# Down-score matmuls of a head quad spread among its local-score matmuls

## The chip, the core and the metric

The kernel runs on one core of a Trainium2 chip. Its engines are PE (matrix multiplication, with a separate record for the loading of weights, PEld), DVE (vector work), ACT (activation functions), POOL (general vector work, and the issue of some DMAs) and SP (the issue of the other DMAs). The metric is the device time of one execution in microseconds (us). All cited lines of code are lines of the kernel before.

## The reference

Eight batches of eight heads with 576 positions of 64 features go through two kinds of attention whose outputs are added. The down attention averages queries, keys and values over groups of four positions, attends over the resulting 144, and repeats each output four times. The local attention lets a position see only positions less than four away. The sum goes, as 4608 tokens of 512 features, through two matrix products with an activation between them.

```
q_d, k_d, v_d = mean over groups of 4 positions
out_up    = repeat(softmax(q_d k_d^T / 8) v_d, 4)
out_local = softmax(where(|i-j| < 4, q k^T / 8, -1e9)) v
x = (out_up + out_local) as 4608 x 512
h = x w_in                                   # 512 -> 2048
out = (h * sigmoid(1.702 h)) w_out           # 2048 -> 512
```

## The kernel before

**Two kinds of work share PE.** The two matrix products run in 9 groups (g = 0 to 8) of 512 tokens. For a group, `mm1` (L702) computes 16 chunks of h, each from 4 matmuls of 512 columns (L687), and ACT applies the activation (`silu`, L698). Then `mm2` (L711) computes 4 blocks of 128 tokens, each from 16 matmuls of 512 columns (L743), and ACT copies each result out (`store`, L728). The attention of batch b = g + 1 is cut into steps that are inserted between these matmuls. Batch 0's attention is done ahead of all groups and by other functions; the diff doesn't change it.

**Steps and places.** `attention` (L644) returns the steps of a batch as a list, and the list `POS` (L772) gives the place of each: places below 16 stand ahead of that chunk of `mm1`, and place 16 + n ahead of the n-th matmul of `mm2`. For g of 1 or more the steps are: score matmuls of quad 0 at 13, their exponentials at 16, scores and exponentials of quad 1 together at 33, the products with the values of head pairs 0 and 1 at 42, of pairs 2 and 3 at 53, and transposes and merges at 62 and 71. Batch 1 runs in group 0 with its own list `POS_0`, where the first steps are at 16, 18 and 27. All engines' orders are as written out in the program: no scheduler moves anything.

**A score burst.** Heads are taken in quads, of which there are two per batch (`qd` 0 and 1). A head's 64 features lie in 32 partitions with two values each (`a` 0 and 1), so a quad's four heads (`r`) fill the four row groups of the PE array. `scores` (L362) computes the local scores in 5 blocks of keys (`i`), each with 2 halves of 64 keys (`par`): 16 matmuls of 32 rows, 64 columns of weights and 60 columns of queries per block, 80 in all. They go to the 8 array tiles in turn, four row groups by two column halves. `scores_d` (L384) computes the down scores in 3 chunks of 48 keys (`kc`): 8 matmuls of 32 rows, 64 columns of weights and 144 columns of queries per chunk, 24 in all. Head r uses only the column half r % 2, so these use 4 of the 8 tiles. Every matmul has a weight load of its own. `s_pe` (L647) issues all 80 local ones and then all 24 down ones.

**Tiles and their release.** Scores go to PSUM, where three double-bank tiles `PA` are handed out in turn by `ps_tile` (L72). A burst takes two for the local scores (`sp`) and a third for the down scores (`sd`). The second burst of a batch takes the same three as the first in the same order, so its local matmuls wait for the exponentials of the first burst's local scores (`exp_local`, L403, two instructions) and its down matmuls for the exponential of the down scores (`exp_down`, L409). ACT runs these three in this order, behind the last activation of `mm1` and the load of a function table (L653). DVE then masks the local ones (L417). The next user of the tiles is `av` (L419), with matmuls at L434 and L456.

**Where the operands come from.** DVE transposes the loaded keys and queries to `kT` and `qT` (L276). POOL averages them to `kdT` and `qdT` (L294, L297), the ones of quad 0 first, then converts the batch's values (L308), then does quad 1, then averages the values (L314, L317). In batch 1 DVE and POOL share the averaging.

Of the kernel before, what the change touches and what calls it, by code (L numbers as in the profile page):

```python
# [19 lines left out]
def kernel(  # L20
# [51 lines left out]
    def ps_tile(n=None):  # L72
        if n is None:
            n = turn["a"] % 3
            turn["a"] += 1
        return PA[n]
# [275 lines left out]
    def bar_others(sp):  # L352
        for r in range(4):
            nc.tensor.matmul(
                sp[r // 2][:, r % 2, 0:300],
                lhsT=id128,
                rhs=off[:, None, :].to_broadcast([128, 5, 60]),
                start=True, stop=True,
                skip_group_check=True,
            )  # L360

    def scores(b, qd, barred=False, sp=None):  # L362
        sp = sp or [ps_tile(), ps_tile()]
        if barred:
            bar_others(sp)
        for i in range(5):
            for a in range(2):
                for par in range(2):
                    for r in range(4):
                        rows = slice(32 * r, 32 * r + 32)  # L370
                        k0 = 114 * i + KSTART[par]
                        q0 = 114 * i + QSTART[par]
                        nc.tensor.matmul(  # L373
                            sp[r // 2][64 * par : 64 * par + 64, r % 2, 60 * i : 60 * i + 60],
                            lhsT=kT[b, qd][rows, k0 : k0 + 64, a],
                            rhs=qT[b, qd][rows, q0 : q0 + 60, a],
                            start=(a == 0 and not barred),
                            stop=(a == 1 or barred),
                            tile_position=(32 * r, 64 * par),
                            skip_group_check=barred,  # L380
                        )
        return sp

    def scores_d(b, qd, sd=None):  # L384
        sd = sd or ps_tile()
        bank = banks(sd)
        for kc in range(3):
            for a in range(2):
                for r in range(4):
                    rows = slice(32 * r, 32 * r + 32)  # L390
                    j = r % 2
                    nc.tensor.matmul(  # L392
                        bank[r // 2][64 * j : 64 * j + 64, SD * kc : SD * kc + SD],
                        lhsT=kdT[qd][rows, 48 * kc : 48 * kc + 64, a],
                        rhs=qdT[b, qd][rows, :, a],
                        start=(a == 0), stop=(a == 1),
                        tile_position=(32 * r, 64 * j),
                    )
        return sd

    def exp_local(qd, sp):
        for u in range(2):
            nc.scalar.activation(  # L403
                out=es[2 * qd + u][:, :, 0:300], in_=sp[u][:, :, 0:300],
                func=AF.Exp, scale=inv_sqrt_d,
            )

    def exp_down(qd, sd):
        nc.scalar.activation(  # L409
            out=eds[qd][:, :, 0:432], in_=sd[:, :, 0:432],  # L410
            func=AF.Exp, scale=inv_sqrt_d / 16.0,
        )

    def mask_local(qd):
        for u in range(2):
            ev = es[2 * qd + u][:, :, 0:300]
            nc.vector.tensor_tensor(out=ev, in0=ev, in1=mask, op=ALU.mult)  # L417

    def av(b, hp, n=None):  # L419
        o = ps_tile(n)  # L420
        av_local(b, hp, o)
        av_down(b, hp, o)
        return o

    def banks(t):
        return t if t is PM else [t[:, u, :] for u in range(2)]
# [37 lines left out]
    def normalise(o):  # L464
        y = work.tile([128, 2, 7, D], BF16, name="y", tag="y", bufs=4)
        rc = work.tile([128, 2, 7, 1], FP32, name="rc", tag="rc")
        for xs in (slice(0, 1), slice(1, 2)) if o is PM else (slice(0, 2),):
            n = xs.stop - xs.start
            ov = (o[xs.start][:, None, :] if o is PM else o)[:, :, 0:455].rearrange(
                "p x (c e) -> p x c e", e=65  # L470
            )
            nc.vector.reciprocal(rc[:, xs], ov[:, :, :, 64:65])  # L472
            nc.vector.tensor_tensor(  # L473
                out=y[:, xs], in0=ov[:, :, :, 0:D],
                in1=rc[:, xs].to_broadcast([128, n, 7, D]), op=ALU.mult,
            )
        return y

    def transp(y, n=None):
        x = ps_tile(n)  # L480
        for i in range(5):
            for par in range(2):
                for j in range(2):
                    pos = j if par == 0 else 1 - j
                    c0 = 0 if (par == 1 or i == 0) else 3
                    c1 = 60 if (par == 0 or i == 4) else 57
                    nc.tensor.matmul(  # L487
                        x[64 * j : 64 * j + 64, par, 57 * i + c0 : 57 * i + c1],
                        lhsT=y[64 * pos : 64 * pos + 60, par, i, :],
                        rhs=ident(pos, 60, c0, c1),  # L490
                        start=True, stop=True,
                        tile_position=(64 * pos, 64 * j),
                    )
        for c2, xx in ((0, 0), (0, 1), (1, 0)):
            for j in range(2):
                pos = j if xx == 0 else 1 - j
                nc.tensor.matmul(  # L497
                    x[64 * j : 64 * j + 64, xx, 288 + 48 * c2 : 336 + 48 * c2],
                    lhsT=y[64 * pos : 64 * pos + 48, j, 5 + c2, :],
                    rhs=ident(pos, 48, 0, 48),  # L500
                    start=True, stop=True,
                    tile_position=(64 * pos, 64 * j),
                )
        return x
# [91 lines left out]
    def copy_od(x):  # L596
        od = work.tile([128, S], FP32, name="od", tag="od")
        for xx, t0, n in ((0, 0, 96), (1, 96, 48)):
            nc.scalar.copy(  # L599
                out=od[:, 4 * t0 : 4 * (t0 + n)].rearrange("p (t f) -> p t f", f=4),  # L600
                in_=x[:, xx, 288 : 288 + n, None].to_broadcast([128, n, 4]),
            )
        return od
# [40 lines left out]
    def attention(b, slots=None):  # L644
        st = {}

        def s_pe(qd):  # L647
            st["s", qd] = scores(b, qd)
            st["d", qd] = scores_d(b, qd)

        def s_act(qd):
            if qd == 0:
                nc.scalar.preload_act_table_set("exp_and_others")  # L653
            exp_local(qd, st["s", qd])
            exp_down(qd, st["d", qd])
            if qd == 1:
                nc.scalar.preload_act_table_set("silu_and_others")
            mask_local(qd)

        def s1():  # L660
            s_pe(1)
            s_act(1)

        def avn(*hps):
            def f():
                for hp in hps:
                    st["o", hp] = av(b, hp, slots and slots[hp % 2])
                for hp in hps:
                    st["y", hp] = normalise(st["o", hp])
            return f  # L670

        def tr(*hps):
            def f():
                for hp in hps:
                    st["x", hp] = transp(st["y", hp], slots and slots[hp % 2])
                for hp in hps:
                    od = copy_od(st["x", hp])
                    merge(b, hp, st["x", hp], od)
            return f

        first = [lambda: s_pe(0), lambda: s_act(0), s1, avn(0, 1)]
        if b == 1:
            return first + [tr(0), tr(1), avn(2, 3), tr(2), tr(3)]
        return first + [avn(2, 3), tr(0, 1), tr(2, 3)]
# [84 lines left out]
        for f in steps.get(n, ()):  # L769
            f()  # L770

    POS = [13, 16, 33, 42, 53, 62, 71]  # L772
    POS_0 = [16, 18, 27, 48, 52, 57, 66, 70, 75]
    VDP_0 = 44

    o, y, x = {}, {}, {}
# [28 lines left out]
    prep_1("k", 0, 0)  # L805
    prep_1("q", 0, 0)
    sp = scores(0, 0, barred=True, sp=PA[0:2])
    exp_local(0, sp)
    pool_1(0, 0, "k", nc.vector)
# [5 lines left out]
    for n in range(22):  # L815
        nc.tensor.matmul(
            PM[1][:, 0:256], lhsT=zero16[:, 0:128], rhs=zero16, start=True, stop=True
        )
    exp_down(0, scores_d(0, 0, PA[2]))
    make_up()  # L820
    sp = scores(0, 1, barred=True, sp=PA[0:2])
# [10 lines left out]
    sd = scores_d(0, 1, PA[2])  # L832
# [38 lines left out]
    for g in range(n_groups):  # L871
        b = g + 1
# [33 lines left out]
        if b < B:  # L906
            for n, f in zip(POS if g else POS_0, attention(b, None if g else (1, 2))):
                steps.setdefault(n, []).append(f)
# [35 lines left out]
```

The softmax here doesn't subtract the row's maximum and nothing guards it: scores larger than these inputs give would overflow.

## Time and profile before

| | |
|---|---|
| Median of 6 runs | 324.87 us (323.12 to 326.85) |
| Profiled execution | 324.37 us, span 322.6 us |
| PE busy | 313.6 us, 97% of the span, granted clock 1.00 |
| Large matmuls (L687, L743 at 512 columns) | 544 + 528, one per 216 ns in a row |
| Local-score matmuls (L373) | 1280, 182 to 213 ns each from start to modelled end |
| Down-score matmuls (L392) | 384, 220 to 251 ns each |
| ACT busy | 184.0 us, 57% |
| DVE, POOL busy | 135.2 and 139.8 us |
| Idle PE for w_out, at 50.97 us | 1.60 us |

The page names lines, engines, and for each group of instructions the tile written, the tiles read, the shape, the count and the mean duration. Matmuls are pipelined and overlap each other, so durations don't add up: what a stretch costs is read from the starts, from the last matmul ahead of it to the first one behind it. A timeline line gives the start and the length of a run of equal instructions, its engine, line, tile and count, and in brackets the idle time ahead of it with what ended it. A window's timeline counts what has started by its end.

### The profile page before, as it was taken

To read this page: it belongs to the slowest core of one execution; us is meant where nothing else is said; L and a number is where in the kernel's file an instruction comes from. 1 tells how busy PE (TensorE), PEld (TensorE's weight loads), DVE (VectorE), ACT (ScalarE), POOL (GpSimd) and SP (SyncE) were. 2 spreads that over 40 slices of the span, in tenths; PEclk is the share of its full clock that TensorE was granted. 3 is DMA by queue.
4 is the path that set the end of the run, shared out by engine and by line. 5 is a ranking of instruction groups with operands and counts; after the bars stand their busy time and mean duration, and the time that the engine had idled before them with its cause. 6 is when DMAs were issued, how large, how long until landed. Compare 5 with 4: busy or idle time off the path is not lost.

```text
span 322.6 us, 10981 instructions
## 1 busy us (share of the span) xinstructions
PE 313.6 (97%) x4916; PEld 158.7 (49%) x4916; DVE 135.2 (42%) x224; ACT 184.0 (57%) x317; POOL 139.8 (43%) x172
## 2 busy tenths in 40 slices
PE   7999998999899999999999999999999999999995
PEld 3664554445544555445544554555445544444444
DVE  6972825912664066605770478036711650000000
ACT  4565771667446674659365936583667556415611
POOL 8964970299008930795059603970197000000000
PEclk9999999999999999999999999999999999999999
DMA  7999999799619941795169715991260110020012
GB/s 123 111 188 211 182 112 203 161 241 252 173 39 195 216 115 67 171 216 140 46 165 213 170 37 142 203 201 50 96 118 3 69 65 3 2 94 36 2 60 70
DMA packets 63550, 40.02 MB, mean 124 GB/s; under 512 B 44048, under 2 KB 54416, under 8 KB 63504
## 3 DMA queue, kind: packets, MB, share of 16 engines
q0 software_dynamic: 18864, 14.95, 32.8%
q1 hardware_dynamic: 44496, 24.32, 30.9%
q8 instruction: 38, 0.62, 0.8%
q14 instruction: 8, 0.07, 0.1%
q10 hardware_dynamic: 144, 0.07, 0.1%
HBM read 44.83 MB, written 9.44 MB: 168 GB/s over the span
## 4 chain that ended last, share of the span: by engine, by line
PE 81%; DMA 10%; POOL 5%; ACT 1%; DVE 1%; issue 1%; POOLq 0%; DVEq 0%
PE pm L687 35%; PE pm L743 34%; DMA qb<-in_q_dram 7%; PE pa L373 3%; DMA w_out_bf<-in_moe_w_out_dram 3%; PE pa L487 2%; PE pa L434 2%; POOL vb L230 2%; PE pa L392 2%; PE pa L456 2%; PE pa L743 1%; PE pm L758 1%; POOL w_in_bf L252 1%; POOL kb L199 1%; PE pa L497 0%
## 5 line engine op out<-in xcount | busy, mean ns | idle before, releaser
L743 PE MATMUL pm<-w_out_bf,gT 128*128 128x512 bf16 x528 | 121.7, 380 | 1.6 <-DMA w_out_bf<-in_moe_w_out_dram 1.6
L687 PE MATMUL pm<-xT,w_in_bf 128*128 128x512 bf16 x544 | 121.1, 379 | 0.0
L698 ACT ACTIVATE gT<-pm 128x512 bf16<-128x512 f32 x136 | 81.0, 598 | 44.6 <-PE pm L687 44.6
L687 PEld LDWEIGHTS <-w_in_bf 128*128 128x128 bf16 x576 | 55.6, 98 | 66.9 <-issue 0.4
L743 PEld LDWEIGHTS <-gT 128*128 128x128 bf16 x560 | 51.6, 98 | 60.7 <-issue 1.8
L417 DVE TENSOR_TENSOR es<-es,mask 128x600 bf16<-128x600 bf16 x28 | 20.2, 735 | 84.0 <-ACT es L403 83.1
L294 POOL TENSOR_TENSOR pq<-kT 128x576 f32<-128x576 bf16 x14 | 16.2, 1159 | 88.0 <-DVE kT L276 87.9
L728 ACT ACTIVATE osb<-pm 128x512 f32<-128x512 f32 (+2 forms) x35 | 20.8, 594 | 40.2 <-PE pm L743 35.9
L599 ACT COPY od<-pa 128x384 f32<-128x384 f32 (+1 forms) x56 | 18.5, 412 | 33.6 <-DVE y L473 18.7
L473 DVE TENSOR_TENSOR y<-pa,rc 128x896 bf16<-128x896 f32 x28 | 30.6, 1091 | 1.0
L620 DVE TENSOR_TENSOR xT<-pa,od 128x570 bf16<-128x570 f32 x28 | 21.1, 753 | 12.9 <-ACT od L599 11.2
L730 DVE TENSOR_SCALAR osb<-pm 128x128 f32<-128x128 f32 x1 | 0.3, 291 | 55.3 <-ACT osb L728 55.3
L314 POOL TENSOR_TENSOR v<-v 112x512 f32<-112x512 f32 x18 | 22.8, 1267 | 0.0
L276 DVE STREAM_TRANSPOSE kT<-kb 128x576 f32<-128x576 f32 x16 | 20.0, 1248 | 5.0 <-DMA kb<-in_k_dram 5.0
L403 ACT ACTIVATE es<-pa 128x600 bf16<-128x600 f32 x32 | 19.7, 667 | 2.4 <-PE pa L373 2.2
L276 DVE STREAM_TRANSPOSE qT<-qb 128x576 f32<-128x576 f32 x16 | 19.8, 1240 | 0.3 <-DMA qb<-in_q_dram 0.2
L230 POOL DMA_DIRECT2D vb<-in_v_dram x20 | 13.7, 701 | 5.6 <-DMA w_in_bf<-in_moe_w_in_dram 3.4
L373 PEld LDWEIGHTS <-kT 32*64 32x64 bf16 x1280 | 12.0, 104 | 7.5 <-issue 6.1
L409 ACT ACTIVATE ed<-pa 128x864 bf16<-128x864 f32 x16 | 14.4, 897 | 2.0 <-PE pa L392 2.0
L294 POOL TENSOR_TENSOR pq<-qT 128x576 f32<-128x576 bf16 x13 | 14.9, 1146 | 0.0
L373 PE MATMUL pa<-qT,kT 32*64 32x60 bf16 x1280 | 13.9, 203 | 0.8 <-DVE qT L276 0.8
L472 DVE RECIPROCAL rc<-pa 128x14 f32<-128x14 f32 x28 | 6.7, 240 | 18.5 <-PE pa L456 18.5
(98 smaller groups left out, 268.0 us busy)
## 6 DMA issues: line engine op xcount, KB each, us to landing
out_dram<-osb SPq DMA_DIRECT2D x35, 256.0 KB, 2.1
vf<-in_v_dram SPq DMA_DIRECT2D x60, 128.0 KB, 4.7
v<-in_v_dram SPq DMA_DIRECT2D x36, 192.0 KB, 4.8
kb<-in_k_dram POOLq DMA_DIRECT2D x16, 288.0 KB, 6.9
qb<-in_q_dram POOLq DMA_DIRECT2D x16, 288.0 KB, 8.0
w_out_bf<-in_moe_w_out_dram POOLq DMA_DIRECT2D x4, 512.0 KB, 14.2
vb<-in_v_dram POOLq DMA_DIRECT2D x20, 64.0 KB, 5.6
w_in_bf<-in_moe_w_in_dram POOLq DMA_DIRECT2D x2, 512.0 KB, 8.3
```

What stands on the lines that cost most here:

```text
L230: nc.gpsimd.dma_start(out=vbs[b % 2][64 * par : 64 * par + 64, i, :, 0:D], in_=bass.AP(tensor=v.tensor, offset=v[b, 0].offset + (114 * i + ...
L276: nc.vector.transpose(out=t32.rearrange("p (i c) -> p c i", c=18), in_=store[b, qd].bitcast(FP32).rearrange("p (c d) -> p c d", c=18),)
L294: eng.tensor_tensor(out=t1, in0=sv[:, :, 0:2, :], in1=sv[:, :, 2:4, :], op=ALU.add)
L314: eng.tensor_tensor(out=t1[0:112], in0=x[:, :, 0:2, :], in1=x[:, :, 2:4, :], op=ALU.add)
L373: nc.tensor.matmul(sp[r // 2][64 * par : 64 * par + 64, r % 2, 60 * i : 60 * i + 60], lhsT=kT[b, qd][rows, k0 : k0 + 64, a], rhs=qT[b, qd] ...
L417: nc.vector.tensor_tensor(out=ev, in0=ev, in1=mask, op=ALU.mult)
L473: nc.vector.tensor_tensor(out=y[:, xs], in0=ov[:, :, :, 0:D], in1=rc[:, xs].to_broadcast([128, n, 7, D]), op=ALU.mult,)
L620: eng.tensor_tensor(out=sub(xT[hp], t0 + 3, (57, 2), (114, 5), (1, 57)), in0=sub(x, 3, (509, 2), (57, 5), (1, 57)), in1=sub(od, 3, (57, 2) ...
L687: nc.tensor.matmul(acc, lhsT=w_in_bf[:, dmc, ffc * 128 : (ffc + 1) * 128], rhs=xT[dmc][:, g * TG : g * TG + TG], start=(dmc == 0), stop=(d ...
L698: nc.scalar.activation(out=gT[:, ffc, :], in_=acc, func=AF.Silu, scale=GELU_SCALE)
L728: eng.activation(out=osb, in_=ap, func=AF.Copy, scale=1.0 / GELU_SCALE)
L743: nc.tensor.matmul(ops[t], lhsT=gT[:, ffc, t * 128 : (t + 1) * 128], rhs=w_out_bf[:, ffc, :], start=(ffc == 0), stop=(ffc == n_ffc - 1),)
```

## The change

A new function `scores_mixed` allocates the same three tiles in the same order and calls `scores` with a table of things to be issued ahead of blocks. Chunk 0 of the down scores stands ahead of local block 0, chunk 1 ahead of block 2 and chunk 2 ahead of block 4. So a burst's order is 8 down, 32 local, 8 down, 32 local, 8 down, 16 local, in place of 80 local and 24 down. It is used by `s_pe`, that is for both quads of batches 1 to 7. Batch 0 calls `scores` and `scores_d` as before. The second quad's step moves from place 33 to 35, two large matmuls later, and in batch 1 from 27 to 30. The first quad's place stays (13, and 16 in batch 1). The order of instructions on ACT, DVE, POOL and SP among each other is as before.

```diff
-    def scores(b, qd, barred=False, sp=None):
+    def scores(b, qd, barred=False, sp=None, ahead={}):
         sp = sp or [ps_tile(), ps_tile()]
         if barred:
             bar_others(sp)
         for i in range(5):
+            if i in ahead:
+                ahead[i]()
             for a in range(2):
...
-    def scores_d(b, qd, sd=None):
+    def scores_d(b, qd, sd=None, kcs=range(3)):
         sd = sd or ps_tile()
         bank = banks(sd)
-        for kc in range(3):
+        for kc in kcs:
...
+    def scores_mixed(b, qd):
+        sp = [ps_tile(), ps_tile()]
+        sd = ps_tile()
+        ahead = {2 * kc: (lambda kc=kc: scores_d(b, qd, sd, [kc])) for kc in range(3)}
+        return scores(b, qd, sp=sp, ahead=ahead), sd
...
         def s_pe(qd):
-            st["s", qd] = scores(b, qd)
-            st["d", qd] = scores_d(b, qd)
+            st["s", qd], st["d", qd] = scores_mixed(b, qd)
...
-    POS = [13, 16, 33, 42, 53, 62, 71]
-    POS_0 = [16, 18, 27, 48, 52, 57, 66, 70, 75]
+    POS = [13, 16, 35, 42, 53, 62, 71]
+    POS_0 = [16, 18, 30, 48, 52, 57, 66, 70, 75]
```

## The prediction

> **What bounds the kernel now.** I read the page first: the shares of busy time, then the chain that ended last. PE is busy for 97% of the span at the full granted clock, and the chain consists mostly of PE, with only short stretches on other engines after 61 us. So a microsecond taken from PE there is a microsecond off the end.
>
> ```profile
> PE 313.6 (97%) x4916; PEld 158.7 (49%) x4916; DVE 135.2 (42%) x224; ACT 184.0 (57%) x317; POOL 139.8 (43%) x172
> PE 81%; DMA 10%; POOL 5%; ACT 1%; DVE 1%; issue 1%; POOLq 0%; DVEq 0%
> ```
>
> Next the timeline of PE in one steady turn, and its start cut by ever longer windows, so that the counts at the line ends say how many matmuls had started by then. First the two bursts of batch 4 with what follows them, then the first burst up to 141.03 and 141.23, then its down part up to 141.58, 141.65 and 141.71:
>
> ```profile
> 140.80 0.84 PE L373 MATMUL pa<-qT,kT 32*64 32x60 bf16 x80
> 141.44 0.59 PE L392 MATMUL pa<-qdT,kdT 32*64 32x144 bf16 x24
> 141.96 2.76 PE L687 MATMUL pm<-xT,w_in_bf 128*128 128x512 bf16 x12
> 148.32 1.00 PE L373 MATMUL pa<-qT,kT 32*64 32x60 bf16 x80
> 149.20 0.58 PE L392 MATMUL pa<-qdT,kdT 32*64 32x144 bf16 x24
> ...
> 140.80 0.33 PE L373 MATMUL pa<-qT,kT 32*64 32x60 bf16 x32
> 140.80 0.64 PE L373 MATMUL pa<-qT,kT 32*64 32x60 bf16 x56
> ...
> 141.44 0.34 PE L392 MATMUL pa<-qdT,kdT 32*64 32x144 bf16 x8
> 141.44 0.40 PE L392 MATMUL pa<-qdT,kdT 32*64 32x144 bf16 x12
> 141.44 0.46 PE L392 MATMUL pa<-qdT,kdT 32*64 32x144 bf16 x16
> ```
>
> Here lies the whole case. The 80 local matmuls take 0.64 us and the 24 down ones 0.52 us, and they are limited by different things. By single records, 32 local ones, already queued, start within 140 ns (8 per 32 ns, one per array tile); the 33rd starts 239 ns after the first, and from there one pair of weight load and matmul comes every 8.33 ns: the array waits for instructions. The down ones go in rounds of 4, one round per 64 ns, because only 4 of the 8 tiles are used and each streams 144 columns (at 512 columns per 216 ns, 61 ns): now instructions wait for the array. From the first start to the last it is 1011 ns; the next 512-column matmul comes 153 ns after that.
>
> Last, who releases the second burst: ACT in the same turn, the wait records of the down line, and one line of PE's timeline in batch 2:
>
> ```profile
> 146.67 1.23 ACT L403 ACTIVATE es<-pa 128x600 bf16<-128x600 f32 x2
> 147.79 0.90 ACT L409 ACTIVATE ed<-pa 128x864 bf16<-128x864 f32 x1
> 148.56 0.62 ACT L728 ACTIVATE osb<-pm 128x512 f32<-128x512 f32 x1
> 149.38 0.67 ACT L403 ACTIVATE es<-pa 128x600 bf16<-128x600 f32 x1 [0.20 <-PE pa L373]
> ...
> L392 PEldq EVENT_SEMAPHORE  x7: 51/51/51, 42.2 to 249.9; - x7
> ...
> 88.37 0.29 PE L456 MATMUL pa<-vd,ed 48*64 48x65 bf16 x11 [0.72 <-issue]
> ```
>
> The first quad's down exponential (L409) ends at 148.69, 0.36 us after the second burst has begun. Its PSUM tile takes the second burst's down scores, hence the separate wait instruction on PE, in 7 bursts, the second ones of batches 1 to 7. The last line is a stall of another kind: PE waits for none of the engines, its next instruction is late.
>
> **The change, part by part.** No matmul, exponential, copy or DMA is added or removed; 14 bursts are reordered, and the second of each batch begins 2 matmuls later (3 for batch 1). SP's and POOL's queues keep their order.
>
> *First burst, mixed.* Three blocks of 8 down pairs stand ahead of 32, 32 and 16 local pairs. 32 pairs are queued at the start: 8 down (two rounds, 128 ns) and 24 local (4 ns each), done by about 225 ns, so pair 33 still comes at 239 ns. If instructions alone limited the rest, pair 104 would start at 239 + 71 x 8.33 = 830 ns. A later down block delays the array: its pairs arrive in 67 ns, and occupy it for 17 + 89 + 64 = 170 (the first round after local ones starts 17 ns late and lasts 89 instead of 64, by the records at 141.44), 103 ns behind. Queued local pairs catch up 8.33 - 4 ns each: block 2 is made up after 24 of its 32 pairs; block 3 has only 16, which make up 69 and leave 34. With some 10 ns for a rougher return to local ones the last start is 875. Against 1011 that is 136 ns. The burst also ends on a 60-column stream instead of 144, 84 x 0.42 = 35 ns less ahead of the next weight load: 171 ns in all. Bounds: 216 ns gained (nothing left behind), or, where the array never catches up, 35 gained and two further changes of kind at 42 ns each paid, 50 ns lost. I take the sum, nearest to the rows of the same instructions.
>
> A rule that speaks against this: the Trainium skill, "TensorE: Matmul & The Clock Gate", Part 3, what overlaps and what doesn't, says that a weight load overlaps a running matmul only in another row group. The down rounds reuse their row groups and repeat in 64 ns, not in 61 plus the 31 between a load's start and its matmul's: for queued loads the trace disagrees. By the rule each round would take 92, a block fall 17 + 92 + 92 - 67 = 134 behind and block 3 leave 65 instead of 34: over 12 bursts 0.4 us less gain.
>
> *Second burst.* Its first instruction is now the one that waits for L409. Starting 2 x 216 ns later, at 148.76 by this turn's times, it meets a release at 148.69 (the semaphore at 148.70): 60 ns of margin. But the wait instruction seems to stop PE's sequencer (its record stands 20 ns ahead of local matmuls issued before it, so it isn't in their queue), and then nothing is queued behind it. Waits in PE's own queue end 42 ns after their semaphore; from the wait instruction to the first matmul it is 107 ns in all seven. So the burst starts 149 ns after the release, 90 ns late, without the 32 queued pairs. From there, 103 x 8.33 less 30 (pairs pile up behind the first load) plus the same 34 + 10 ns: last start 872 + 90 = 962 after the undelayed start. Before, without the irregular stalls below, it was 1079 (the wait instruction costs 77 inside the burst). Saved 117 + 35 = 152 ns. Bounds: 286 gained (no late start, nothing left behind); or, since in three bursts, this turn's among them, the first down matmul came 490 to 505 ns after the release, a start 340 later than mine, 188 lost, and 221 more if the array never catches up. Four of seven bursts were as quick as PE reached the wait, so I take the 149.
>
> *Who waits for it.* Local exponentials now start after the whole second burst: the last local matmul at 148.76 + 0.96 = 149.72, and 0.22 later the exponential, at 149.94 instead of 149.38. The two take 1.23 us, until 151.17. They release the PSUM tiles of the next values' matmuls (L434), which begin at 151.76, here up to 0.31 earlier: covered by 0.3 us, and by more for the second of the two tiles; what is late beyond that would come on top in each batch. The masks (L417) after them are wanted only at 155.06. Ahead of the first burst POOL had finished its pooled keys and queries 6 us early (101.29 for the burst at 107.06): bringing the down part forward waits for nothing.
>
> *Batch 1.* Behind its bursts PE waits 1.60 us for w_out to land, at 50.97. What they gain makes that wait longer: 0, and the same for a loss below 1.6 us.
>
> *Sum.* 6 x (171 + 152) = 1.94 us. The profiled execution takes 324.37 us (span 322.6); it would take 322.4. It lies 0.5 below the median of 324.87, so I forecast 322.9.
>
> **Rivals.**
> 1. *The array, not the issue, bounds the mixture.* The tiles of the down matmuls carry local ones too, and order is kept; if nothing catches up, both kinds take what they took. For: the round of 89 ns. Against: 8 starts per 32 ns whenever 32 are queued. Each first burst gains its 35, each second one 77 - 90 + 35 = 22: 0.3 us, 324.5.
> 2. *The wait takes the gain's place.* If release to matmul takes 0.49 us, second bursts lose 340 ns against my sum, 6 x 0.34 = 2.04: 325.0, no change. For: three of seven bursts. Against: they may be stalls of the next kind, and the wait instruction itself takes 51 ns, 107 with its followers, each time.
> 3. *Slower: issue stalls.* PE's instructions sometimes arrive late. Batches 2 to 7 show 0.13, 0.33, 0.91, 0.18, 0.20, 0.16, 0.14 and 0.46 us, 2.5 in all, 0.42 per batch, in or soon after bursts of small matmuls. The mixture draws 208 instructions at the full rate, where the down rounds let them pile up, and leaves 7 instead of 9 large matmuls before the next burst. If each batch had 1.0 us of it, the time would be 6 x 0.6 - 1.94 = 1.7 longer: 326.5. It decides from 0.6 us more per batch, over twice what there is. An extra 0.15 leaves 323.8.
> 4. *Better than the sum.* Nothing left behind and no late start: 6 x 0.50 = 3.0: 321.9.
>
> **How the numbers follow.** About 0.5%, 1.6 us, is what a measurement of this kernel can tell from no change. My sum 0.47, rival 1 0.18, rival 2 0.13, rival 3 0.12, rival 4 0.10. My sum lies not far past 1.6 us, so a fifth of its chance falls within; half of rival 3 stays within its bound, and 0.05 of rival 2 goes with longer waits past it. Faster 0.38 + 0.10 = 0.48; slower 0.06 + 0.05 = 0.11; same 0.41. My sum's own range is 322.2 to 323.8 (12 bursts, some 50 ns either way each, and a little for the runs' scatter). The whole range runs from 0.5 below rival 4 to between rivals 2 and 3: 321.4 to 325.8.
>
> **What the changed profile would show.** First bursts with the last start near 875 ns after the first and the next 512-column matmul some 120 later; second bursts starting about 0.40 us after the last large matmul instead of 0.31, and all PE issue stalls near 2.5 us. Wrong if first bursts still last 1.0 us (rival 1), if second ones begin 0.7 us after the last large matmul (rival 2), or if large issue stalls appear ahead of L434 and L456 (rival 3).

## The result, and the profile after

The changed kernel takes 327.57 us (median of 19 runs, 325.32 to 332.33) against 324.57 us (38 runs): the ratio is 1.0085, with an interval of 1.0065 to 1.0105. It is slower by 0.85%, 2.8 us, where a gain of 1.9 was forecast. In some executions the granted clock drops for a while; they widen the spreads given here and count in no ratio.

The profiled execution of the changed kernel took 325.32 us (span 323.5) and a second one 325.89 (span 324.1). Before, the two profiled executions took 324.37 (span 322.6) and 323.94 (span 322.2). So the traces show 1.0 to 2.0 us of the loss of 2.8, and what is explained below is that part.

The page of the changed kernel: busy time of PE, the DMA queue that brings instructions (packets, MB, share of 16 engines), and the chain that ended last.

```profile
PE 312.5 (97%) x4916; PEld 158.2 (49%) x4916; DVE 134.9 (42%) x224; ACT 184.0 (57%) x317; POOL 140.1 (43%) x172
...
q8 instruction: 38, 0.62, 0.8%
...
PE 91%; DMA 4%; issue 2%; DVE 1%; POOL 1%; ACT 0%; POOLq 0%; DVEq 0%
```

PE is *less* busy than before (312.5 against 313.6 us) in a longer span, so the loss is idle time. The chain's "issue" has gone from 1% to 2%. The queue q8 is one that the prediction never looked at.

Did the bursts get shorter? PE's timeline of the changed kernel in batch 4, both bursts: the last large matmul ahead, the first matmuls, the last down block with what follows, and the next large matmul.

```profile
140.82 0.38 PE L694 MATMUL pm<-xT,w_in_bf 128*128 128x512 bf16 x1
141.13 0.26 PE L394 MATMUL pa<-qdT,kdT 32*64 32x144 bf16 x4
...
141.51 0.27 PE L394 MATMUL pa<-qdT,kdT 32*64 32x144 bf16 x4
...
141.88 0.27 PE L394 MATMUL pa<-qdT,kdT 32*64 32x144 bf16 x4
...
142.21 0.60 PE L694 MATMUL pm<-xT,w_in_bf 128*128 128x512 bf16 x2
...
148.70 0.38 PE L750 MATMUL pm<-w_out_bf,gT 128*128 128x512 bf16 x1
149.08 0.26 PE L394 MATMUL pa<-qdT,kdT 32*64 32x144 bf16 x4
...
150.16 1.04 PE L750 MATMUL pm<-w_out_bf,gT 128*128 128x512 bf16 x4
```

They did. From the start of the last large matmul to the start of the next, the first burst takes 1.39 us (142.21 less 140.82) where it took 1.47, and the second 1.46 where it took 1.54 undisturbed and about 1.69 with its irregular stalls. Summed over batches 2 to 7 the first bursts save 0.44 us (8.53 against 8.96) and the second ones 0.60 (9.12 against 9.72), together 1.04. In the second pair of executions they save 0.84.

Where the loss is: the same timeline in batches 2, 3, 5 and 6, where the values' matmuls stand (L442 and L464; they were L434 and L456).

```profile
84.71 0.25 PE L464 MATMUL pa<-vd,ed 48*64 48x65 bf16 x6 [1.41 <-issue]
...
119.14 0.28 PE L464 MATMUL pa<-vd,ed 48*64 48x65 bf16 x8 [0.55 <-issue]
...
186.37 0.32 PE L464 MATMUL pa<-vd,ed 48*64 48x65 bf16 x15 [0.74 <-issue]
...
220.82 0.35 PE L464 MATMUL pa<-vd,ed 48*64 48x65 bf16 x18 [0.69 <-issue]
```

PE's waits in batches 2 to 7 (line, what was waited for, us in all, times, longest), after:

```profile
PE pa L464 <- issue: 3.4, 4, 1.4
```

and before, in the first and in the second execution:

```profile
PE pa L456 <- issue: 1.0, 2, 0.7
```

```profile
PE pa L456 <- issue: 2.4, 4, 1.0
```

Idle time is counted from the modelled end of the matmul before, some 0.19 us late. Taken from start to start, the four stalls after are 1.60, 0.73, 0.92 and 0.87 us, 4.12 together, and before they were 1.90. The loss of 2.22 and the gain of 1.04 make 1.18 us; the stretch from the start of group 1 to the start of group 7 is longer by 1.20 (204.25 against 203.05). That balance is closed. Ahead of it the changed kernel is 0.23 us *faster*, so the span differs by 0.97. In the second pair the stalls grow by 1.70, the bursts give 0.84 back, and groups 1 to 6 are 0.98 longer; there the span differs by 1.95, since group 0 is longer by another 0.83, which is batch 1's (end of this section).

**What the stalls are.** The records of q8 are 38 transfers of 16384 bytes, one after the other over the whole span. PE's stalls fall behind matmul 1374, 1502, 2014, 3165 and 3804. Counted in instructions (weight loads, matmuls, and the few waits and drains among them) that is 2753, 3009, 4033, 6337 and 7617, all exactly 256 n - 63: one transfer brings 256 instructions, which is 128 pairs of weight load and matmul. Where PE stalls in batches 2 to 7, the block's transfer has started 0.4 to 2.4 us after PE entered the block before it (up to 3.3 at the second of batch 2's block ends), takes 0.88 to 1.9 us, and the next instruction starts 1.1 to 1.6 us after the transfer's end. In sum the next block begins 3.1 to 4.7 us after PE entered the one before it (up to 5.5 at that second end): no fixed time. 128 pairs of 512 columns take 27.6 us, and the wait is long over; but in four batches a block ends inside the second score burst, and the next one 128 pairs on, in the first of the values' bursts. For batch 2:

```
block end, in matmuls           before   after
PE passes 1246 (score burst)     80.00   80.17
transfer starts                  81.13   81.92
transfer ends                    82.43   83.25
PE has used up the block         83.48   83.10
first matmul of the next block   83.82   84.71
```

The change shortens the burst and takes two large matmuls out from behind it: the block is used up 2.93 us after PE enters it instead of 3.48. That is 0.55 of the 1.27 us by which this stall grew. The next 0.62 is that the transfer starts later, 1.75 us after PE enters instead of 1.13, and that isn't the change's doing: in the second executions it is 1.87 before and 1.10 after.

A stall is the difference between the time until a block is used up and the time until the next one's first instruction, both counted from PE's entry into the block. Batch 5 apart (see below the table of stalls), only the first moved with the change. By the starts of weight loads, in batches 2, 3, 5 and 6, a block lasts PE 3.5, 3.5, 3.4 and 3.6 us before, and 2.9, 2.8, 2.8 and 2.8 after, within 0.04 in both executions. The time to the next block's first instruction, where PE stalled there, was 3.8 to 4.7 us before and 3.5 to 4.7 after, and it scatters by as much as 1 us between executions of one kernel.

One more line of the changed kernel is new, in batch 1, whose second burst was moved from place 27 to 30 (PE's timeline):

```profile
45.06 2.75 PE L750 MATMUL pa<-w_out_bf,gT 128*128 128x512 bf16 x12 [0.92 <-ACT es L411]
```

A block of `mm2` that uses one of the scores' PSUM tiles now waits 0.92 us for an exponential. The wait of 1.60 us for w_out in the same batch, on which the prediction counted as a cover, stands in the first execution of before alone. PE's waits from 36 to 62 us, in the second execution of before and in the changed kernel:

```profile
PE pa L487 <- DVE y L473: 0.2, 1, 0.2
```

```profile
PE pa L750 <- ACT es L411: 0.9, 1, 0.9
PE pa L495 <- DVE y L481: 0.2, 1, 0.2
```

Group 0 takes 38.62 and 37.31 us before, 38.08 and 38.14 after. So where w_out lands in time, batch 1 costs about 0.8 us, nearly half of what the second pair of spans shows.

### The profile page after: what moved, and what is told of

The parts are those of the page before. It is cut to its first block, busy times and chain, and to the rows that moved or that the text cites. A ratio compares the mean times of both kernels' runs of the same rounds, so it can differ in the third digit from the quotient of the medians.

```text
span 323.5 us, 10980 instructions
## 1 busy us (share of the span) xinstructions
PE 312.5 (97%) x4916; PEld 158.2 (49%) x4916; DVE 134.9 (42%) x224; ACT 184.0 (57%) x317; POOL 140.1 (43%) x172
## 4 chain that ended last, share of the span: by engine, by line
PE 91%; DMA 4%; issue 2%; DVE 1%; POOL 1%; ACT 0%; POOLq 0%; DVEq 0%
PE pm L694 37%; PE pm L750 36%; PE pa L375 3%; PE pa L750 2%; PE pa L694 2%; DMA qb<-in_q_dram 2%; PE pa L394 2%; PE pa L495 2%; PE pa L442 2%; PE pa L464 2%; DMA vb<-in_v_dram 2%; PE pm L765 1%; DVE y L481 1%; PE pa L581 1%; PE pa L505 0%
## 5 line engine op out<-in xcount | busy, mean ns | idle before, releaser
L375 PE MATMUL pa<-qT,kT 32*64 32x60 bf16 x1280 | 17.5, 199 | 1.2 <-DVE qT L276 1.2
L375 PEld LDWEIGHTS <-kT 32*64 32x64 bf16 x1280 | 15.9, 103 | 1.7 <-issue 1.4
L394 PE MATMUL pa<-qdT,kdT 32*64 32x144 bf16 x384 | 15.4, 231 | 0.0
```

Of the source, the lines that this page charges most:

```text
L375: nc.tensor.matmul(sp[r // 2][64 * par : 64 * par + 64, r % 2, 60 * i : 60 * i + 60], lhsT=kT[b, qd][rows, k0 : k0 + 64, a], rhs=qT[b, qd] ...
L394: nc.tensor.matmul(bank[r // 2][64 * j : 64 * j + 64, SD * kc : SD * kc + SD], lhsT=kdT[qd][rows, 48 * kc : 48 * kc + 64, a], rhs=qdT[b, q ...
```

## The experiments

The prediction's own rivals left three causes for the loss: the instructions' arrival, the wait for the down exponential at the head of the second burst, and the places (35 and 30 instead of 33 and 27). The first four runs take the change apart. Stalls, here and in the table at the end, are starts beyond the usual step at the five block ends named above, in one profiled execution.

**Places alone.** The order of before, with the new places:

```diff
-    POS = [13, 16, 33, 42, 53, 62, 71]
-    POS_0 = [16, 18, 27, 48, 52, 57, 66, 70, 75]
+    POS = [13, 16, 35, 42, 53, 62, 71]
+    POS_0 = [16, 18, 30, 48, 52, 57, 66, 70, 75]
```

> The order of before (80 local, then 24 down matmuls), with the changed places (second burst at 35, in batch 1 at 30). Three theories. Late instructions: PE's instructions come in blocks of 256 (16 KB), and in batches 2, 3, 5 and 6 the values' burst reaches the end of a loaded block before the next one has landed; what counts is the time from the second score burst to that point. Two large matmuls fewer in between are 0.43 us, so the four stalls at L456 should grow by 0.43 each, 1.7 us in all: about 326.3. PSUM wait in batch 1: a wait of up to 1.1 us at the first large matmul into a pa tile, part of which the later wait for w_out takes back: 324.6 to 325.7. Mixed burst costly in itself: nothing happens here, 324.6.

Measured: 323.88 us against 323.70, ratio 1.0003 (0.9985 to 1.0020). Stalls are 2.19 us, between the 1.90 and 3.14 of the two profiles of before. Against the first of these the first stall in batch 2 and those in batches 3 and 6 are 0.34 to 0.41 us longer, which is what two large matmuls less (0.43) would make them, but the second profile of before has them as long or longer. The second bursts lost their irregular stalls of about 0.15 us (all last 1077 to 1080 ns from first start to last). The places alone cost nothing in sum. They do shorten the time that a block lasts PE, from 3.5 to 3.0 us in batches 3 and 6, and the mixture alone (next run) shortens it to 3.2; together it is 2.8. So both edits have a part in it.

**Mixture alone.** The mixed order at the old places:

```diff
-    POS = [13, 16, 35, 42, 53, 62, 71]
-    POS_0 = [16, 18, 30, 48, 52, 57, 66, 70, 75]
+    POS = [13, 16, 33, 42, 53, 62, 71]
+    POS_0 = [16, 18, 27, 48, 52, 57, 66, 70, 75]
```

> The mixed order with the places of before (33 and 27). The second burst's first instruction now waits for the down exponential, which ends 0.36 us after the burst's old start, and begins 0.15 after that. Late instructions: stalls at L464 stay within 0.4 us of before's 1.9 in sum, since the distance to the values is again 9 large matmuls; the wait adds 0.51 per second burst, less 0.13 and 0.03 for the shorter burst, and first bursts give 0.08 back: 6 x 0.27 = 1.6 us more than before, about 326.2. PSUM wait in batch 1: the wait of 0.92 us at 45.06 shrinks to under 0.5. Mixed burst costly in itself: the whole loss stays, 327.3.

Measured: 327.68 us, ratio 1.0115 (1.0082 to 1.0148). PE's timeline in batch 2:

```profile
78.81 0.81 PE L750 MATMUL pm<-w_out_bf,gT 128*128 128x512 bf16 x3
80.06 0.26 PE L394 MATMUL pa<-qdT,kdT 32*64 32x144 bf16 x4 [0.43 <-ACT ed L417]
```

Every second burst starts 0.815 us after the last large matmul's start, 0.505 later than undisturbed. Stalls are 3.27 us. So the order needs the later place: without it, each of the six batches pays half a microsecond of waiting, and the stalls come on top.

**Batch 1 back.** The changed kernel with `POS_0` as before (27 instead of 30), to see whether the 0.92 us at 45.06 cost anything:

```diff
-    POS_0 = [16, 18, 30, 48, 52, 57, 66, 70, 75]
+    POS_0 = [16, 18, 27, 48, 52, 57, 66, 70, 75]
```

> The changed kernel, with batch 1's second burst back at place 27, all else as changed. PSUM wait in batch 1: PE's wait of 0.92 us for the exponential goes down by some 0.5 us (three large matmuls earlier, less the wait for the down exponential), and 0 to 0.5 us of it is seen at the end, the rest being taken by the wait for w_out: 326.9 to 327.4. Late instructions and mixed burst: no change from the changed kernel, 327.4, stalls at L464 about 4 us in sum.

Measured: 326.59 us, ratio 1.0091 (1.0054 to 1.0127), no better than the change itself. Nor is group 0 (38.57 us), because the earlier place has waits of its own:

```profile
PE pa L394 <- ACT ed L417: 0.5, 1, 0.5
...
PE pa L750 <- ACT es L411: 0.3, 1, 0.3
```

The second burst waits 0.5 us for the down exponential and the block of `mm2` another 0.3: one wait has been exchanged for two. So this run doesn't show that the 0.92 us cost nothing.

**Values two places later.** The changed kernel with nine large matmuls between second burst and values, as before the change:

```diff
-    POS = [13, 16, 35, 42, 53, 62, 71]
+    POS = [13, 16, 35, 44, 53, 62, 71]
```

> The changed kernel, with the first values' burst of batches 2 to 7 moved from place 42 to 44, so that 9 large matmuls lie between it and the second score burst again. Late instructions: four stalls shorter by 0.43 us each, 1.7 us in all: about 325.7, the stalls at L464 down to some 2.4 us in sum. The other two theories: no change, 327.4.

Measured: 325.45 us, ratio 1.0054 (1.0025 to 1.0082). The time may come back in part (the intervals of the two ratios overlap), but the stalls of the profiled execution are 4.43 us, no less than the change's 4.12: 1.60 in batch 2 became 1.18, by about the 0.43 expected of two matmuls, while batch 5's grew from 0.92 to 1.32. In batches 3, 5 and 6 the blocks did last PE 0.42 us longer, 3.2 us instead of 2.8, but the next ones came 0.2 to 0.8 us later than in the changed kernel's first profile. One execution scatters as much as this: the second profile of the changed kernel has 0.76, 0.95, 1.19 and 1.85 us where the first had 1.60, 0.73, 0.92 and 0.87. So one profile can't tell 0.43 us a batch, and whether the stalls hang on the places in the schedule or on positions in the instruction stream needed a test of another kind.

**64 pairs ahead.** If block ends are what counts, moving all bursts against them must move the stalls, with nothing changed behind the start. Sixty-nine small matmuls, whose results nobody uses, replace 5 of the 22 warming ones at the start; everything behind stands 64 pairs later in the stream:

```diff
-    for n in range(22):
+    for n in range(17):
         nc.tensor.matmul(
             PM[1][:, 0:256], lhsT=zero16[:, 0:128], rhs=zero16, start=True, stop=True
         )
+    for n in range(69):
+        r, j = n % 2, n // 2 % 2
+        rows = slice(32 * r, 32 * r + 32)
+        nc.tensor.matmul(
+            PM[r][64 * j : 64 * j + 64, 0:60],
+            lhsT=zero16[rows, 0:64], rhs=zero16[rows, 0:60],
+            start=True, stop=True, tile_position=(32 * r, 64 * j),
+        )
```

> The changed kernel with 64 more pairs of weight load and small matmul ahead of batch 0 (69 small ones on zeros in place of 5 of the 22 warming matmuls, about the same time; the results are not used). That moves every later instruction by half a block of 256, and nothing else. Instruction blocks: the four large stalls leave batches 2, 3, 5 and 6 and appear where the block's end now falls in both bursts, in batches 4 and 7, with at most small ones in others; their sum goes from some 4.1 us to 2 to 2.5, the time to 325.4 to 326.0. If the stalls belong to the bursts themselves (PSUM, waits, the mixed order): they stay in the same batches, no change of time.

PE's timeline of this kernel in batch 4, which has no such stall in any other kernel run here:

```profile
160.09 0.29 PE L442 MATMUL pa<-vb,es 64*64 64x65 bf16 x13 [0.95 <-issue]
```

The stalls of batches 2, 3, 5 and 6 are gone. Instead there is one of 1.14 us in batch 4, and 0.33 and 0.11 us in batch 7. Groups 1 to 6 take 201.6 us against the change's 204.3, and 203.0 before. This settles that the stalls belong to positions in the instruction stream. The kernel isn't faster (326.48 us, ratio 1.0070, 1.0035 to 1.0104): block ends now fall into the bursts of batches 0 and 1, with stalls of 1.60, 2.25 and 2.14 us there, and this execution then lost more at a halved clock (last section).

**Down blocks ahead of local blocks 2, 3 and 4.** Thirty-two local pairs stand first, so the wait for the down exponential is no longer the burst's first instruction:

```diff
-        ahead = {2 * kc: (lambda kc=kc: scores_d(b, qd, sd, [kc])) for kc in range(3)}
+        ahead = {kc + 2: (lambda kc=kc: scores_d(b, qd, sd, [kc])) for kc in range(3)}
```

> The changed kernel with the down chunks ahead of local blocks 2, 3 and 4 in place of 0, 2 and 4: 32 local matmuls stand first, and the wait for the down exponential comes behind them. Instruction blocks: PE can again take in the first instructions of the second burst during the large matmuls, so in batch 5, where a block ends 9 pairs into that burst, the next load starts early and its stall of 0.9 to 1.5 us goes; second bursts start 0.31 instead of 0.38 after the last large matmul; together 1.4 to 2.0 us less than the changed kernel: 325.4. The other three stalls stay. Mixed burst costly in itself: no change, 327.2.

Measured: bursts are far shorter. First bursts take 1320 ns from large matmul to large matmul (changed: 1390; before: 1473). In first and second bursts alike the last start comes 885 ns after the first, and the second ones start 309 ns after the last large matmul: no wait is left at the head. Stalls are 2.10 us, none in batch 5. The profiled execution took 321.29 us (span 319.5), but the timed ones have a median of 323.18, ratio 1.0003 (0.9973 to 1.0034): against the change it is a gain, against before it can't be told from none.

**Before, values three places later.** The stalls without any change of order:

```diff
-    POS = [13, 16, 33, 42, 53, 62, 71]
+    POS = [13, 16, 33, 45, 56, 62, 71]
```

> The kernel before with both values' bursts of batches 2 to 7 three large matmuls later (45 and 56). Instruction blocks: 0.65 us more between the second score burst and the values, so the stalls at L456 (0.20, 0.33 and 0.46 us in the profile of before, and the 0.91 between the two values' bursts less surely) go: 1.0 to 1.6 us less than before, 322.4. If stalls don't hang on that distance: 323.7 as before.

Measured: 321.99 us, ratio 0.9970 (0.9940 to 1.0001). Stalls fall to 1.22 us; the stretch of groups 1 to 6 is 202.0 us against 203.0 and 204.2 in the two profiles of before. Three large matmuls more after the score burst help the kernel before, too, by this profile; the interval of the timed runs just reaches 1.

**First bursts alone mixed,** at the old places:

```diff
         def s_pe(qd):
-            st["s", qd], st["d", qd] = scores_mixed(b, qd)
+            if qd == 0:
+                st["s", qd], st["d", qd] = scores_mixed(b, qd)
+            else:
+                st["s", qd] = scores(b, qd)
+                st["d", qd] = scores_d(b, qd)
...
-    POS = [13, 16, 35, 42, 53, 62, 71]
-    POS_0 = [16, 18, 30, 48, 52, 57, 66, 70, 75]
+    POS = [13, 16, 33, 42, 53, 62, 71]
+    POS_0 = [16, 18, 27, 48, 52, 57, 66, 70, 75]
```

> Mixed order in the first burst of each batch alone, second bursts and places as before. Instruction blocks: the first bursts become 80 ns shorter as in the changed profile, no value burst follows them within a block, and the second bursts are untouched: 0.5 us less than before, 323.2 where before is 323.7. Mixed burst costly in itself: half of the loss, about 1.4 us more than before.

Measured: the profiled execution took 322.20 us with 0.98 us of stalls, so mixing the first bursts does no harm there. The timed runs spread from 321.99 to 326.39, median 323.84, ratio 1.0032 (0.9996 to 1.0067): inconclusive.

**Both together.** Down blocks from block 2, batch 1's place as before, and the values four and three places later:

```diff
-        ahead = {2 * kc: (lambda kc=kc: scores_d(b, qd, sd, [kc])) for kc in range(3)}
+        ahead = {kc + 2: (lambda kc=kc: scores_d(b, qd, sd, [kc])) for kc in range(3)}
...
-    POS = [13, 16, 35, 42, 53, 62, 71]
-    POS_0 = [16, 18, 30, 48, 52, 57, 66, 70, 75]
+    POS = [13, 16, 35, 46, 56, 62, 71]
+    POS_0 = [16, 18, 27, 48, 52, 57, 66, 70, 75]
```

> Down chunks ahead of local blocks 2, 3 and 4, second burst at place 35 (27 in batch 1), and the values' bursts of batches 2 to 7 at 46 and 56. Instruction blocks: the gain of the bursts stays (309 + 885 + 126 = 1320 ns for a first burst, against 1472 before: 0.15 us each, 12 bursts, 1.8 us), and the stalls at L464, 2.1 us in sum where only the down chunks were moved, go to about 0.5, since there are 11 large matmuls in between instead of 7: 1.8 + 1.4 less than before, 320.6. If the stalls don't hang on the distance: 1.8 less than before at most, and stalls of 2 us.

Measured: 321.32 us against 323.69, ratio 0.991 (0.988 to 0.994). It beats both kernels. PE's timeline of its second burst in batch 4:

```profile
147.23 0.38 PE L750 MATMUL pm<-w_out_bf,gT 128*128 128x512 bf16 x1
147.54 0.33 PE L375 MATMUL pa<-qT,kT 32*64 32x60 bf16 x32
147.78 0.28 PE L394 MATMUL pa<-qdT,kdT 32*64 32x144 bf16 x5
...
148.34 0.29 PE L375 MATMUL pa<-qT,kT 32*64 32x60 bf16 x13
148.56 0.82 PE L750 MATMUL pm<-w_out_bf,gT 128*128 128x512 bf16 x3
```

Thirty-two local matmuls start in 0.24 us, the first down one joins without a wait, and the next large matmul comes 1.33 us after the last. Over batches 2 to 7 the bursts save 2.72 us against the first profile of before and stalls (1.53 us) another 0.37, and its groups 1 to 6 are 3.09 us shorter.

**The change with the values as late as that,** to separate the two edits:

```diff
-    POS = [13, 16, 35, 42, 53, 62, 71]
+    POS = [13, 16, 35, 46, 56, 62, 71]
```

> The changed kernel with the values' bursts of batches 2 to 7 four and three places later (46 and 56), nothing else. Instruction blocks: 0.86 us more between the second score burst and the values; each of the four large stalls of the changed profile (1.60, 0.73, 0.92, 0.87) shrinks by up to that: 3.3 us less than the changed kernel, stalls at L464 0.7 in sum, 324. Mixed burst costly in itself: 327.

Measured: 323.40 us, ratio 0.998 (0.9949 to 1.0011). PE's waits in batches 2 to 7:

```profile
PE pa L464 <- issue: 1.4, 2, 0.8
PE pa L442 <- issue: 0.5, 2, 0.3
```

Stalls are down to 2.64 us from the change's 4.12 and 4.84, and the loss of the change is gone. Groups 1 to 6 take 203.0 us, where the change took 204.3 and 205.2. So their loss was made of these stalls, and large matmuls ahead of the values take them up. What is left of them stands at the same block ends.

**Both kernels a second time,** one profiled execution each beside these runs, unchanged.

> The changed kernel once more, for a second profile: the first profiled execution was among the fastest of its runs. Instruction blocks: the same four places (matmuls 1374, 2014, 3166 and 3806 counted from the start), 4 to 6 us in sum.

> The kernel before once more, for a second profile. Instruction blocks: stalls at the same matmuls but 3166, 1.5 to 2.5 us in sum.

Measured: 325.89 us after, with 4.84 us of stalls; 323.94 before, with 3.14. So stalls differ by 0.7 to 1.2 us between executions of the same kernel, and the two kernels still stand apart. The second pair of groups 1 to 6: 205.2 and 204.2 us.

All stalls at one sight, in us, but for the kernel with 64 pairs ahead, whose block ends lie elsewhere; "wait first" tells whether the second burst begins with the wait for the down exponential, and the last columns give the profiled execution and the median with its ratio to before:

| kernel | wait first | batch 2 | batch 2, next block | 3 | 5 | 6 | sum | profiled | median, ratio |
|---|---|---|---|---|---|---|---|---|---|
| before | no | 0.33 | 0.91 | 0.20 | 0 | 0.46 | 1.90 | 324.37 | 324.57 |
| before again | no | 1.22 | 0.64 | 0.47 | 0 | 0.81 | 3.14 | 323.94 | |
| changed | yes | 1.60 | 0 | 0.73 | 0.92 | 0.87 | 4.12 | 325.32 | 327.57, 1.0085 |
| changed again | yes | 0.76 | 0.09 | 0.95 | 1.19 | 1.85 | 4.84 | 325.89 | |
| places alone | no | 0.67 | 0.09 | 0.61 | 0 | 0.82 | 2.19 | 323.45 | 323.88, 1.0003 |
| mixture alone | yes | 1.12 | 0.37 | 0.76 | 0.54 | 0.48 | 3.27 | 327.34 | 327.68, 1.0115 |
| batch 1 back | yes | 1.66 | 0 | 0.75 | 1.47 | 0.74 | 4.62 | 326.04 | 326.59, 1.0091 |
| values at 44 | yes | 1.18 | 0.51 | 0.79 | 1.32 | 0.63 | 4.43 | 325.68 | 325.45, 1.0054 |
| down from block 2 | no | 0.22 | 0.36 | 0.65 | 0 | 0.87 | 2.10 | 321.29 | 323.18, 1.0003 |
| before, values at 45 | no | 0 | 0.92 | 0.30 | 0 | 0 | 1.22 | 322.12 | 321.99, 0.997 |
| first bursts alone | no | 0 | 0 | 0.74 | 0 | 0.24 | 0.98 | 322.20 | 323.84, 1.0032 |
| block 2, values at 46 | no | 0 | 0.50 | 0.80 | 0 | 0.23 | 1.53 | 321.26 | 321.32, 0.991 |
| changed, values at 46 | yes | 0.80 | 0 | 1.01 | 0.37 | 0.46 | 2.64 | 323.85 | 323.40, 0.998 |

Batch 5 is the cleanest column: a stall stands there in all six profiles in which the wait heads the second burst, and in none of the seven others. The block that it needs starts to load, against the moment when PE passes matmul 3037, six to eight pairs into the burst: 1.03 to 1.49 us after it in those six, and from 1.71 us *before* it to 0.8 after it in the seven. The reading that fits both: where the burst begins with local matmuls, PE takes in the block's last instructions ahead of executing them, and the transfer is asked for early; a wait instruction at the head keeps it from that. That reading is argued from these times; no record shows PE taking instructions in.

## Why the prediction was wrong

**The step that failed is the treatment of the issue stalls.** The sum left all 2.5 us of them as they were, and rival 3 gave the right mechanism a chance of 0.12: the mixture draws its instructions faster, seven large matmuls instead of nine stand behind the second burst, and the stalls would come ahead of L434 and L456. That is where they are. At the block ends they rose from 1.90 and 3.14 us to 4.12 and 4.84, about 2.0 us in the mean, which is more than the bursts gave. The evidence lay in the profile of before. The line with 0.72 us at 88.37 was quoted, and its cause was not looked for; the positions of the stalls in the count of matmuls, and the 38 transfers on the queue for instructions, would have shown that 128 pairs have a price in time of their own, and so that where PE already stalls at such an end, whatever is taken out ahead of it is handed back as a stall. The prediction priced the two large matmuls less at nothing; with four of them put back behind the second burst the stalls fall to 2.64 us and the loss is gone, and three more in the kernel before bring its own down to 1.22.

**The wait instruction was costed at 90 ns a batch, for its late start alone.** That was right (384 against 309 ns to the large matmul ahead: 75 late). That nothing is queued behind it is not shown: in the changed kernel's batch 4, 33 pairs of the second burst start within 248 ns and the next one at 278, where the first burst has 32 within 227 and the next at 278, too. What was missed is that with the wait at the head the next block is asked for later, by the reading above because the same stop holds up the intake of instructions: batch 5's 0.92 and 1.19 us.

**First bursts: the last start was to be at 875 ns and is at 956 to 960** in six of the twelve in the two profiles, and at 1014 to 1063 in the others. The term that was mis-sized is the pace at the head. Pair 33 comes 278 ns after the first instead of 239 in the burst at 141.13, and the 40 pairs from one down block to the next take 372 ns, 9.3 each, not 8.33 made up by queued ones. With 32 local pairs first, the same kind of mixture gives 885: the assumption that queued pairs catch up holds there. Second bursts were to last 872 and last 951 to 960 where nothing disturbs them (eight of twelve). What follows the last start was put at 118 ns and is 121 to 126 in these bursts. In all the bursts of batches 2 to 7 gave 1.04 us of the 1.94, and 0.84 in the second pair of executions.

**The rivals.** Rival 1 (the array bounds the mixture, first bursts gain 35 ns) is out: they gain 80. Rival 2 (release to first matmul in 0.49 us) is out as it was put: the change starts its second bursts 75 ns late, because of the places; at the old places the wait does cost 0.505 us. Rival 4's size (3.0 us) is nearly met by the kernel with the values later and the down blocks from block 2.

**Batch 1** was costed at nothing, with the w_out wait as its cover. That term failed, too. The cover is no property of the kernel: the second profile of before and the one with the values later, where batch 1 runs the same program, have no such wait, and group 0 takes 37.31 and 37.30 us in them. The new wait of 0.92 us for a PSUM tile was put at nothing without a look at who uses the tiles next, and group 0 of the changed kernel is about 0.8 us longer than these two. That the first pair of profiles shows a gain there instead is luck: of all the profiles here, that one alone waits for w_out.

**What stays open.** The traces show 1.0 to 2.0 us of a loss of 2.8. Timed runs of the changed kernel lie on median 1.7 to 2.2 us above its two profiled executions, and those of the kernel with down blocks from block 2 lie 1.9 above its one. Stalls differ between executions by as much as 1 us at a single block end, so longer ones in the others would do it; no trace of such an execution shows that. Nor is it known how often PE waits for w_out in the timed runs, and so how much of the 2.8 is batch 1's. What sets the moment at which a block's transfer starts is open as well, and with it the scatter of the stalls. Of the 2.0 us by which they rose in the mean, 1.06 are batch 5's and go with the wait at the head. The other 0.9, in batches 2, 3 and 6, is no larger than the scatter between two executions; that blocks last PE 0.5 to 0.8 us less there is beyond it.

## What to carry to other kernels

Before reordering bursts of small matmuls, count where the stalls stand in the stream of instructions: if they repeat at a fixed count, instructions arrive in blocks that each take their time, and shortening a burst only pays if enough long instructions stand between one block end and the next. Put an instruction with a separate wait behind others that are ready, rather than at the head of such a burst. Look at a second profile before a wait is taken as a cover. And a stall that the profile puts down to nothing is a term of the sum like any other: find its cause before assuming that it stays.

## What the runs showed of the hardware

**Instructions come in blocks of 16384 bytes, and crossing a block isn't free.** The Trainium skill, "Runtime: NRT & Kernel Launch", section "Instruction fetch mechanics", states blocks of 16 KiB or 256 instructions, fetched by a DMA queue of the sequencer's own, at a cost that is mostly hidden, since instructions are issued more slowly than they are fetched. The transfers agree with the size: 16384 bytes for 128 pairs. The cost differs in this kernel: pairs start every 4 to 9 ns in a burst, the next block begins 3.1 to 4.7 us after PE has entered the one before it, and single stalls reach 1.85 us (2.25 in the kernel with 64 pairs ahead).

**Two stalls of over 2 us were followed by a halved clock for longer than they lasted.** The kernel with 64 pairs ahead stalled for 2.25 us until 20.27. The table of stretches of that kernel (columns: us, busy time of PE and its matmuls, of PEld, DVE, ACT and POOL, then the granted clock, DMA share, GB/s):

```profile
18.00:20.00 2.00, 0.23 (x13) 0.06 (x2) 1.20 (x3) 0.21 (x1) 1.13 (x2) 1.00 1.21 197
...
22.00:24.00 2.00, 2.00 (x39) 1.34 (x32) 1.93 (x8) 0.82 (x1) 2.00 (x1) 0.50 1.14 217
...
30.00:31.00 1.00, 1.00 (x4) 0.30 (x2) 0.00 (x0) 0.20 (x1) 0.39 (x1) 0.50 1.10 205
31.00:32.00 1.00, 1.00 (x11) 0.65 (x9) 0.00 (x0) 0.00 (x0) 0.68 (x1) 0.94 1.07 199
```

The granted clock is 0.50 from 20.9 us until 31.1, and again for 3.4 us behind the stall of 2.14 us that ends at 51.58. Stalls of up to 1.85 us in the other kernels were followed by no such drop. By an estimate from these times, 10.2 us at half the clock cost up to 5.1 us of work, about twice the stall itself. Both cases stand in one execution, so that the stalls are the cause is likely, not shown.
